# A planned kernel on one core: new planner constants, start times and nudges, with the same instructions

## The chip, the core and the metric

The kernel runs on one core of a Trainium2 chip. The metric is the device time of one execution in microseconds (us), as a median over runs. The engines are TensorE (PE, with its weight loads PEld), VectorE (DVE), ScalarE (ACT), GpSimd (POOL) and SyncE (SP, which here only issues DMAs; POOL issues some too).

## What is computed

A linear-attention block gated by a mixer MLP, for 2048 tokens of width 512, in float32:

```python
x = A_x
xn = _layernorm(x)
s = _A_ref(xn, wqkv, wo)                    # 32 heads of 16, linear attention
g = _silu(_B_ref(xn, w1, w2, w3, w4))       # token shifts and an MLP of 1376
return x + s * g
```

```python
# _A_ref: phi(t) = where(t > 0, t + 1, exp(t)) + 1e-6
kv = einsum("bhsd,bhse->bhde", phi(k), v); z = sum over s of phi(k)
o = einsum(phi(q), kv) / (einsum(phi(q), z) + 1e-6);  return o @ wo
# _B_ref
h = _gelu(_layernorm(x) @ w1)
hs = concat of the four column quarters of h, shifted by +1, -1, +2, -2 tokens, @ w2
x1 = x + hs
return x1 + _gelu(_layernorm(x1) @ w3) @ w4
```

## The kernel before

**Arithmetic.** Each float32 operand is split into a high and a low part for the PE's fp32r format, and each product is three matmuls (hi x hi, lo x hi, hi x lo). Names such as u_0h and u_0l or w_0h and w_0l are such pairs: usually ACT rounds the high part and DVE subtracts to get the low part. Large products are made in seven partial products instead of eight (function `seven`, L890): the banks `pa`, `pb` and `pe` are written by groups of six matmuls (two chunks of three), ACT or DVE takes the sum out, and the next group accumulates further into the same bank. So TensorE cannot go on in a bank before the reader of the last group is done; it computes other groups meanwhile. Functions that use this form are the second mixer product (`mix2`), the up and down products of the MLP (`up_pair`, which reads weight forms that `load_form` fetches from DRAM) and the products of q with kv and wo (`attend_pair`).

**Stages of the span.** From 0 to 44 us: k and q projections of the first tokens, Gram products for the row statistics, and the layernorm's fold into the weights; from 44 us `mix1` (L927, bank `h`: normalized x times w1, which needs the scaled weights w_0h and so on), then alternately k/q work, `mix2`, and later, block by block (four blocks of 512 tokens), the MLP (up, then down into bank `a`) and the attention. `chain` (L1324) adds the residual to a block's MLP sum, `gate` (L1430) makes silu, multiplies by the attention (`th`), adds x and stores.

The end of the head has this path: means are transposed on PE and written to DRAM as one row (`mrow`), fetched back spread over all partitions (`um`, SP), subtracted from x transposed (`xt`, DVE), and sums over it make the correction that DVE adds to the w1 weights (`w_s`); ACT rounds that to w_0h, and the first `h` matmul can start. The term w1 arrives in `w1t` by a load from SP and three accumulating gathers from POOL into the same tile. `rs` is a row of reciprocal roots, made on POOL by a power (`power`, L608/L611); `kr` on ACT reads it.

**What sets the order.** Nothing is written out by hand. The program code adds operations to a `Plan` (L88) in program order, each with its engine, its busy time, its latency, and what it reads and writes; `deadlines` and `backward` (L269) give each a due time from the nominal sequence of matmuls, and `emit` (L275) puts them out: it keeps a clock per engine and, again and again, takes the operation that can start first; among those within .02 us (PE) or .08 us (others) the one due first. It follows the tile slots (98 pieces, 8 PSUM banks), the port that DVE and POOL share, the loaded ACT table and, with `landing` (L228), when a DMA will have landed. These numbers only set the order of instructions on each engine, and which buffer a tile gets; on the chip the engines run by semaphores. A table `SOONER` (L1696) moves the due times of single operations, by number, in quarters of a us.

Lines that the rows below name: all matmuls are issued from L148, ACT from L170, DVE's tensor-tensor operations from L192, its scalar ones from L197 and L202, SP's loads from L212, its stores from L216, its fetches from L220, and POOL's gathers (DMAs that add into their target) from L224. In the changed file these lines stand at the same numbers up to L224, and up to six lines lower behind.

The rules of `emit` that the change touches (`r` is the time at which a reader `o` of the operation `op` is ready; the last line is from `landing`):

```python
free = {e: 0.0 for e in avail}
...
if o.eng == e == "PE" and not flow:
    r = 0.0
elif o.eng == e:
    r = op.end
else:
    r = op.end + self.GAP
...
dma = max(dma, s + (.33 if soft else 0)) + op.mb * op.rate
```

Of the kernel before, what the change touches and what calls it, by code (L numbers as in the profile page):

```python
# [14 lines left out]
P = 128  # L15
# [66 lines left out]

class Op:
    __slots__ = ("eng", "busy", "lat", "emit", "pre", "post", "tiles", "opens", "two", "table", "patience", "soon", "loads",
                 "nom", "due", "ready", "at", "end", "mb", "order", "rate")


class Plan:  # L88
# [9 lines left out]
    def add(self, eng, busy, lat, reads, writes, emit, two=False, table=None, mb=0.0):  # L98
        op = Op()
        op.eng, op.busy, op.lat, op.emit, op.two, op.table, op.mb = eng, busy, lat, emit, two, table, mb  # L100
        op.pre, op.post, op.tiles, op.opens = {}, [], {}, False
        op.order = len(self.ops)
        op.patience, op.soon, op.rate = self.patience, False, 0.0
# [55 lines left out]
    def act(self, out, src, func, scale=1.0, bias=None, total=None):  # L159
        nc = self.nc  # L160
        psum = out.tile.psum or src.tile.psum
        lat = (.15 if psum else .195) + out.n / 1200
        lat += .092 * (isinstance(scale, View) + isinstance(bias, View)) + (.095 if total is not None else 0)
        table = {AF.Exp: 0, AF.Gelu_apprx_tanh: 1, AF.Silu: 2}.get(func)

        def emit():
            kw = {} if bias is None else {"bias": get(bias)}
            if total is not None:
                kw["accum_out"] = total.get()
            nc.scalar.activation(out.get(), src.get(), func, scale=get(scale), **kw)  # L170

        self.add("ACT", lat - .1, lat, [src, scale, bias], [out] + ([] if total is None else [total]), emit, table=table)
# [31 lines left out]

    def move(self, eng, out, src, kind, mb, reads, writes, emit):
        op = self.add(eng, .42 if eng == "SP" else .6, 0, reads, writes, emit, mb=mb)
        op.rate = self.RATE[kind]
        return op

    def load(self, out, src):  # L210
# [11 lines left out]
    def gather(self, out, src, share=1.0):  # L222
        return self.move("POOL", out, src, "gather", out.n * P * 4 / 1e6 * share, [src, out], [out],
                         lambda: self.nc.gpsimd.dma_start(out.get(), get(src), accum_op=ALU.add))  # L224

    RATE = {"load": 2.92, "fetch": 3.5, "row": 4.18, "turn": 5.7, "store": 2.44, "gather": 5.79}

    def landing(self, op, s, dma):  # L228

        soft = op.eng == "POOL"  # L230
        dma = max(dma, s + (.33 if soft else 0)) + op.mb * op.rate
        late = min(1.11, .68 * max(0.0, dma - s))
        return dma, max(dma + (1.36 if soft else 1.25) + late, s + (3.77 if soft else 1.97 if op.loads else 1.68))

    GAP = .06
    PATIENCE = 2.5
    COLD, COLD_TILL = 1.84, 5.8
    SAFE = 2.0
# [30 lines left out]
    def backward(self):  # L269
        for op in reversed(self.ops):  # L270
            if op.eng != "PE":
                for o in op.post:
                    op.due = min(op.due, o.due - self.GAP - (6.0 + op.mb * 4 if op.mb else op.lat))

    def emit(self, first, lead, reserve, window, ahead, table=()):  # L275
        self.deadlines(first)
# [7 lines left out]
                avail[op.eng].append(op)  # L284
        pe = [op for op in ops if op.eng == "PE"]
        head = 0
        free = {e: 0.0 for e in avail}
        slots = {tag: [(0.0, i) for i in range(n)] for tag, n in self.counts.items()}
        port, dma = 0.0, 0.8
        lock = [(-1.0, -1.0)] * 8  # L290
        under = [0.0] * 8, [0.0] * 8
        table = 0
# [3 lines left out]
        while left:  # L296
# [5 lines left out]
            for e, cands in avail.items():  # L302
                picks = []
                low = INF
                for op in cands:
                    s = max(free[e], op.ready)
                    if op.mb:
                        s = max(s, under[e == "POOL"][0] + self.GAP)
                    if op.two and s < port:
                        s = port  # L310
                    if e == "POOL" and not op.mb and not op.two:
                        s = next((b + .02 for a, b in lock if a <= s < b), s)
                    if op.table is not None and op.table != table:
                        s = max(s, free[e] + 1.28)
                    ok = True
                    fresh = [t for t in op.tiles if t.ap is None]
                    for t in fresh:
                        if t.tag not in slots:
                            continue
                        q = slots[t.tag]  # L320
# [4 lines left out]
                        s = max(s, q[need - 1][0] + self.GAP)  # L325
                        if e == "PE":
                            if op is not front and (len(q) < 2 or op.nom - front.nom > ahead):
                                ok = False
                                break
                        elif t.tag in lead:  # L330
                            n = lead[t.tag] * (1.5 if len(q) > reserve[t.tag] else 1)
                            if t.tag == "p":
                                n = min(n, SCARCE * (len(q) - need + 1))
                            s = max(s, op.due + slip - n - t.early)
                    if not ok:
                        continue
                    if e == "PE" and op.nom - front.nom > window:
                        continue
                    q = s
                    if op.table is not None and op.table != table and op.due + slip < s:  # L340
                        q = s - 1.28
                    picks.append((q, s, op))
                    low = min(low, q)
                if not picks:
# [7 lines left out]
            s, op = best  # L352
# [30 lines left out]
            for o in op.post:  # L383
                flow = o.pre[op]
                if o.eng == e == "PE" and not flow:
                    r = 0.0
                elif o.eng == e:
                    r = op.end
                else:
                    r = op.end + self.GAP  # L390
                if op.mb:
                    r = max(r, min(r + self.SAFE, o.due + slip - o.lat - self.SAFE))
                o.ready = max(o.ready, r)
# [8 lines left out]
def linear_attn_gated_by_mixer(  # L402
# [744 lines left out]
    def load_form(b, s, name):  # L1147
# [6 lines left out]
        else:  # L1154
# [1 line left out]
            o = d * TH  # L1156
            pl.fetch(in2(t.f32), w4d[s + r * NS].cut(
                [(o, o + TH), (o + 512, o + 512 + TH)], 512,
                lambda ap, o=o: ap.rearrange("p (k w) -> p k w", k=2)[:, :, o:o + TH]))
        G4[b, s, name] = t.cols(0, TH), t.cols(TH, 512)  # L1160

    def load_group(b, s):
# [161 lines left out]
    def chain(b, n):  # L1324
# [8 lines left out]
        for k in (("11",), ("12",), ("21", "22"))[n]:  # L1333
# [1 line left out]
            o = h * 1024 + d * TH  # L1335
            x1 = x1d[b].cut([(o, o + TH), (o + 512, o + 512 + TH)], 512, lambda ap, h=h, d=d: quarter_of(ap, h, d))
            pl.act(e[k], t.all, AF.Copy)
            pl.gather(in2(e[k]), x1)

    def quarter_of(ap, h, d):  # L1340
        return ap[2 * h * P:2 * (h + 1) * P, d * TH:(d + 1) * TH].rearrange("(j p) c -> p j c", p=P)
# [88 lines left out]
    def gate(b, h, d, a, o=0, w=512, xr=None, whole=False):  # L1430
# [8 lines left out]
        pl.tt(th, th, so, ALU.mult)  # L1439
        j0, j1 = o // TH, (o + w) // TH  # L1440
        if xr is None:
            pl.gather(in2(th), quarter(x, b, h, d, j0, j1))
# [170 lines left out]
    for b in range(NQ):  # L1613
# [80 lines left out]
                gate(b, 1, 0, r, j * TH, TH, xr=xr[1, 0], whole=j > 0)  # L1694

    SOONER = (  # L1696
# [4 lines left out]
    )  # L1701
    pl.emit(first=6.0, lead={"p": 14.0, "w": 14.0}, reserve={"p": 20, "w": 1}, window=12.0,
            ahead=6.0, table=SOONER)
# [37 lines left out]
```

## Time and profile before

| | us |
|---|---|
| median of 3 runs | 510.47 (510.02 to 511.31) |
| the profiled execution | 510.98 |
| its span, first to last instruction | 509.2 |
| granted TensorE clock | 1.000 |
| DMA moved | 115.67 MB, 227 GB/s on average |

The profiled execution is one execution with a recorder on; every row below is from it. Row forms: in the timeline, start, duration, engine, line, operation, result <- operands, shapes, how many; in square brackets the idle time of the engine just before and what released it. A matmul's duration is modelled, and successive ones overlap: what it costs is the distance to the next start, 0.232 us for 512 columns and 0.118 us for 256 at full rate. A DMA row of SP or POOL is the issue, not the transfer. The span is 1.8 us shorter than the execution's time; the rest is start and end outside of the records.

### The profile page before, as it was taken

How to read it: one execution, taken by the hardware profiler on the slowest of the kernel's cores; microseconds unless marked ns; L12 is line 12 of the kernel's file. 1: busy time of each engine (PE TensorE's matmuls, PEld its weight loads, DVE VectorE, ACT ScalarE, POOL GpSimd, SP SyncE). 2: the span in 40 equal slices, each digit the busy share in tenths (PEclk: the TensorE clock that was granted, in tenths of full speed). 3: DMA queues.
4: the chain of work that ended last, by engine and by line, in shares of the span. 5: the costliest groups of instructions: out<-in, count | busy, mean ns of one | idle time of the engine just before them, and what ended most of it. 6: DMA issues, size and time to landing. Idle time of an engine off the chain costs nothing.

```text
span 509.2 us, 9828 instructions
## 1 busy us (share of the span) xinstructions
PE 500.7 (98%) x3287; PEld 453.0 (89%) x3287; DVE 443.6 (87%) x945; ACT 374.3 (74%) x756; POOL 106.6 (21%) x157
## 2 busy tenths in 40 slices
PE   8998999999999999999999999999999999999996
PEld 6776877898888888889999999999999999999996
DVE  5989999999699985999999996977789869999564
ACT  5899688765797785867767688846597667987561
POOL 1276402363243122021000020300030300032100
PEclk9999999999999999999999999999999999999999
DMA  7989956369994799989875989989699897899905
GB/s 266 315 172 216 306 172 166 65 148 285 273 312 105 220 308 217 255 215 313 297 229 171 309 260 310 215 213 242 228 213 294 199 236 216 270 226 256 246 7 122
DMA packets 90895, 115.67 MB, mean 227 GB/s; under 512 B 8800, under 2 KB 50044, under 8 KB 90844
## 3 DMA queue, kind: packets, MB, share of 16 engines
q1 hardware_dynamic: 78668, 98.00, 60.9%
q0 software_dynamic: 12176, 17.04, 21.2%
q8 instruction: 26, 0.43, 0.3%
q14 instruction: 25, 0.20, 0.1%
HBM read 73.70 MB, written 32.91 MB: 209 GB/s over the span
## 4 chain that ended last, share of the span: by engine, by line
PE 93%; DMA 3%; ACT 2%; DVE 1%; SPq 0%; issue 0%; ACTq 0%
PE a L148 15%; PE pb L148 11%; PE h L148 9%; PE g L148 7%; PE pbk L148 7%; PE acc L148 6%; PE pe L148 6%; PE pbm L148 5%; PE pbs L148 5%; PE uc L148 3%; PE pek L148 3%; PE pa L148 3%; PE pem L148 2%; PE pes L148 2%; PE k L148 2%; PE pak L148 2%
## 5 line engine op out<-in xcount | busy, mean ns | idle before, releaser
L224 POOL DMA_DIRECT2D th<-in_x x14 | 15.5, 1468 | 173.6 <-DMA w4t<-w_0h 60.6
L170 ACT ACT_TABLE_LOAD x26 | 33.4, 1283 | 5.8 <-DMA w4t<-w_1l 2.3
L224 POOL DMA_DIRECT2D e<-x1d x12 | 14.4, 1302 | 56.8 <-ACT e L170 27.1
L224 POOL DMA_DIRECT2D o<-x x16 | 13.8, 860 | 50.6 <-DVE o L192 35.5
L224 POOL DMA_DIRECT2D zacc<-kr x16 | 14.3, 894 | 44.2 <-DVE kr L202 21.3
L170 ACT ACTIVATE gf<-gf 128x256 f32<-128x256 f32 (+1 forms) x48 | 22.0, 466 | 0.5
L611 POOL TENSOR_TENSOR rs<-w,nhalf 128x4 f32<-128x4 f32 (+2 forms) x10 | 11.5, 1149 | 29.3 <-DVE w L197 28.4
L202 DVE SCALAR_TENSOR_TENSOR kr<-kt,kr 128x512 f32<-128x512 f32 x16 | 10.9, 686 | 5.8 <-ACT kt L170 5.8
L170 ACT ACTIVATE ht<-ht 128x512 f32<-128x512 f32 x16 | 9.6, 624 | 6.9 <-DVE ht L192 6.8
L170 ACT ACTIVATE th<-e 128x512 f32<-128x512 f32 (+1 forms) x12 | 7.2, 612 | 8.7 <-DVE e L192 8.7
L192 DVE TENSOR_TENSOR e<-a,e 128x512 f32<-128x512 f32 (+1 forms) x12 | 7.6, 663 | 6.7 <-PE a L148 6.7
L605 DVE BATCH_NORM_STATS2 st<-o 128x6 f32<-128x512 f32 x16 | 10.8, 685 | 3.1 <-DMA o<-x 3.1
L170 ACT ACTIVATE x<-x,nm,rs 128x512 f32<-128x512 f32 x16 | 12.9, 807 | 0.0
L192 DVE TENSOR_TENSOR th<-th,so 128x512 f32<-128x512 f32 (+1 forms) x17 | 10.7, 652 | 2.5 <-ACT th L170 2.5
L170 ACT ACTIVATE y<-o,nm,rs 128x512 f32<-128x512 f32 x16 | 12.1, 809 | 0.7 <-DVE nm L202 0.7
L202 DVE SCALAR_TENSOR_TENSOR pq<-pq,qr 128x512 f32<-128x512 f32 x12 | 8.1, 686 | 4.4 <-ACT pq L170 4.4
L170 ACT ACTIVATE p<-pb 128x256 f32<-128x256 f32 x20 | 7.5, 375 | 5.9 <-PE pb L148 5.8
L192 DVE TENSOR_TENSOR ht<-h,abc 128x512 f32<-128x512 f32 x16 | 11.0, 686 | 0.4 <-PE h L148 0.3
L192 DVE TENSOR_TENSOR gf<-u,pe 128x256 f32<-128x256 f32 x20 | 8.2, 412 | 3.5 <-PE pe L148 3.4
L202 DVE SCALAR_TENSOR_TENSOR pq<-pq,rd 128x512 f32<-128x512 f32 x16 | 11.0, 690 | 0.2
L170 ACT ACTIVATE p<-pe 128x256 f32<-128x256 f32 x20 | 7.6, 380 | 4.9 <-PE pe L148 4.9
L192 DVE TENSOR_TENSOR gf<-pa,p 128x256 f32<-128x256 f32 x20 | 8.3, 415 | 3.3 <-PE pa L148 3.2
(1820 smaller groups left out, 2362.1 us busy)
## 6 DMA issues: line engine op xcount, KB each, us to landing
w_s<-in_w SPq DMA_DIRECT2D x34, 256.0 KB, 4.4
w_t<-w4t SPq DMA_DIRECT2D x26, 256.0 KB, 5.3
w_b<-w4d SPq DMA_DIRECT2D x24, 256.0 KB, 4.7
x<-in_x SPq DMA_DIRECT2D x16, 256.0 KB, 5.4
zacc<-kr POOLq DMA_DIRECT2D x16, 256.0 KB, 5.1
o<-x POOLq DMA_DIRECT2D x16, 256.0 KB, 4.5
x1d<-o SPq DMA_DIRECT2D x16, 256.0 KB, 3.6
xt<-in_xt SPq DMA_DIRECT2D x15, 256.0 KB, 5.2
```

Source lines behind the costliest of these rows:

```text
L148: lambda: nc.tensor.matmul(out.get(), lhs.get(), rhs.get(), start=start, stop=stop, skip_group_check=more))
L170: nc.scalar.activation(out.get(), src.get(), func, scale=get(scale), **kw)
L192: self.vec(eng, out, [a, b], lambda: self.e(eng).tensor_tensor(out.get(), a.get(), b.get(), op=op), True)
L202: lambda: self.nc.vector.scalar_tensor_tensor(out.get(), a.get(), get(s), b.get(), op0=op0, op1=op1),
L224: lambda: self.nc.gpsimd.dma_start(out.get(), get(src), accum_op=ALU.add))
L605: pl.add("DVE", .62, .69, [xv], [st], lambda: nc.vector.bn_stats(st.get(), xv.get()))
L611: lambda: g.tensor_tensor(out.get(), src.get(), nh.get(), op=ALU.pow))
```

## The change

Only the planner's numbers and rules are changed. It adds no arithmetic and takes none away, and the operations that the program code adds are the same.

```diff
-        lat = (.15 if psum else .195) + out.n / 1200
+        lat = (.165 if psum else .195) + out.n / 1200
...
-        op.rate = self.RATE[kind]
+        op.rate, op.tail = self.RATE[kind], self.TAIL.get(kind, 0.0)
...
-    RATE = {"load": 2.92, "fetch": 3.5, "row": 4.18, "turn": 5.7, "store": 2.44, "gather": 5.79}
+    RATE = {"load": 2.93, "fetch": 3.3, "half": 4.27, "row": 4.23, "turn": 5.4, "store": 2.45,
+            "gather": 5.73, "quarter": 6.42}
...
-        return dma, max(dma + (1.36 if soft else 1.25) + late, s + (3.77 if soft else 1.97 if op.loads else 1.68))
-
-    GAP = .06
+        return dma, max(dma + (1.36 if soft else 1.25) + late, s + (3.77 if soft else 1.97 if op.loads else 1.68)) + op.tail
+
+    GAP = {"PE": .16, "ACT": .035, "DVE": .035, "POOL": .15, "SP": .035}
+    BEGIN = {"PE": 1.0, "ACT": 2.0, "DVE": .8, "POOL": .8, "SP": .75}
+    DMA0 = 2.2
+    TABLE = 1.41
+    TAIL = {"row": .95}
...
-                    op.due = min(op.due, o.due - self.GAP - (6.0 + op.mb * 4 if op.mb else op.lat))
+                    op.due = min(op.due, o.due - self.GAP[o.eng] - (6.0 + op.mb * 4 if op.mb else op.lat))
...
-        free = {e: 0.0 for e in avail}
+        free = dict(self.BEGIN)
...
-        port, dma = 0.0, 0.8
+        port, dma = 0.0, self.DMA0
...
-                        s = max(s, free[e] + 1.28)
+                        s = max(s, free[e] + self.TABLE)
...
-                elif o.eng == e:
+                elif o.eng == e and not flow:
                     r = op.end
                 else:
-                    r = op.end + self.GAP
+                    r = op.end + self.GAP[o.eng]
...
-            pl.gather(in2(e[k]), x1)
+            pl.gather(in2(e[k]), x1, kind="quarter")
...
     SOONER = (
-        9, 64, 23, 58, 119, -8, 132, 2, 183, 4, 269, -8, 291, 8, 333, 72, 336, 16, 357, 2, 394, -4, 412, -32,
...
+        23, 4, 35, 8, 49, 4, 55, 2, 61, 4, 131, 3, 132, -6, 143, 2, 181, 8, 183, 4, 211, 2, 256, 64, 273, -4,
...
```

`GAP` is the lag that the planner puts between the end of an operation and the start of one that reads it. It was .06 us for all; now it goes by the reader's engine, .16 for TensorE and .035 for ACT, DVE and SP, and it also holds between an operation and its reader on the same engine. `load_form`'s fetches are of the new kind "half", the gathers of `chain` and `gate` of the new kind "quarter". `TAIL` makes the rows that are spread over the partitions land .95 us later in the plan. `BEGIN` starts the engines' clocks at times of their own. The `SOONER` table goes from 37 pairs to 57, 12 of which are as before.

Three places show what the new order moves. The first is the start of SP's queue, where weights (wk_s, first factor of k) and x transposed (xt) are loaded. Before:

```order
L212 DMA xt_0_99<-in_xt 128x256
L212 DMA wk_s_105<-in_wqkv 128x512
L212 DMA xt_0_99<-in_xt 128x256
L212 DMA wk_s_113<-in_wqkv 128x512
L212 DMA xt_1_117<-in_xt 128x512
L212 DMA wk_s_123<-in_wqkv 128x512
L212 DMA xt_2_127<-in_xt 128x512
L212 DMA wk_s_131<-in_wqkv 128x512
L212 DMA xt_3_134<-in_xt 128x512
```

And in the changed kernel:

```order
L212 DMA xt_0_98<-in_xt 128x256 x2
L212 DMA wk_s_107<-in_wqkv 128x512
L212 DMA wk_s_112<-in_wqkv 128x512
L212 DMA xt_1_116<-in_xt 128x512
L212 DMA wk_s_122<-in_wqkv 128x512
L212 DMA xt_2_126<-in_xt 128x512
L212 DMA w1t<-in_w 128x512
L212 DMA wk_s_134<-in_wqkv 128x512
L212 DMA xt_3_136<-in_xt 128x512
```

The load of w1t now stands ahead of the last wk_s and the last xt. On POOL, at the same time of the program, the first of the w1t gathers stood alone ahead of the powers that make rs; in the changed kernel two stand there:

```order
L224 DMA w1t<-in_w 128x512 x2
L616 TENSOR_TENSOR rs_92<-w_315,nhalf 128x1
L616 TENSOR_TENSOR rs_92<-w_361,nhalf 128x2
L224 DMA w1t<-in_w 128x512
L719 CAST u_0h<-hal 128x2
```

DVE begins with wk_0h and wk_0l instead of u_0h and u_0l, which now come fourth and eighth. On ACT, the operations sq (sums of squares of x rows) move ahead: two stand ahead of wneg and one more ahead of kr.

The second place is on TensorE in the MLP of the last block: bank pe_0 of the first pair, from its group with yt13 to the next with yb223. Before:

```order
L148 MATMUL pe_0_6281<-yt13h,w_0_s0l 128x256
L148 MATMUL pb_0_6255<-yt23h,w_0_s0h 128x256
L148 MATMUL pb_0_6255<-yt23l,w_0_s0h 128x256
L148 MATMUL pb_0_6255<-yt23h,w_0_s0l 128x256
L148 MATMUL pb_0_6255<-yt23h,w_0_s0h 128x256
L148 MATMUL pb_0_6255<-yt23l,w_0_s0h 128x256
L148 MATMUL pb_0_6255<-yt23h,w_0_s0l 128x256
L148 MATMUL pe_0_6281<-yb223h,w_0_s1h 128x256
```

And in the changed kernel, the last rows of the same piece:

```order
L148 MATMUL pb_0_6257<-yt23h,w_0_s0h 128x256
L148 MATMUL pb_0_6257<-yt23l,w_0_s0h 128x256
L148 MATMUL pb_0_6257<-yt23h,w_0_s0l 128x256
L148 MATMUL pb_1_6306<-yb113h,w_1_ah 128x256
L148 MATMUL pb_1_6306<-yb113l,w_1_ah 128x256
L148 MATMUL pe_0_6281<-yb223h,w_0_s1h 128x256
```

Between the two groups that use pe_0 stood six matmuls, and now eight: two of the next pair's first group are drawn ahead.

The third place is the end of SP's queue, with the stores of the last gates (th300 and th301, th310 and th311 are the two halves of two row groups; xr is a loaded part of x, which th311 gets by a gather instead). Before:

```order
L216 DMA out_0<-th300_0_7150 128x2x256
L216 DMA out_0<-th311_0_7213 128x2x256
L216 DMA out_0<-th301_0_7249 128x2x256
L216 DMA out_0<-th310_0_7268 128x256
L216 DMA out_0<-th310_256_7284 128x256
```

And in the changed kernel:

```order
L216 DMA out_0<-th300_0_7153 128x2x256
L216 DMA out_0<-th301_0_7248 128x2x256
L216 DMA out_0<-th311_0_7212 128x2x256
L216 DMA out_0<-th310_0_7268 128x256
L216 DMA out_0<-th310_256_7284 128x256
```

The store of th301 has moved ahead of that of th311.

More of the change, by code (lines that the diff above doesn't have):

```diff
@@ L84 @@
     __slots__ = ("eng", "busy", "lat", "emit", "pre", "post", "tiles", "opens", "two", "table", "patience", "soon", "loads",
-                 "nom", "due", "ready", "at", "end", "mb", "order", "rate")
+                 "nom", "due", "ready", "at", "end", "mb", "order", "rate", "tail")
 class Plan:
@@ L102, in add @@
         op.order = len(self.ops)
-        op.patience, op.soon, op.rate = self.patience, False, 0.0
+        op.patience, op.soon, op.rate, op.tail = self.patience, False, 0.0, 0.0
         op.loads = any(isinstance(v, View) and v.tile.tag != "dram" for v in writes)
@@ L220, in fetch, with gather @@
                          lambda: self.nc.sync.dma_start(out.get(), src.get()))
-    def gather(self, out, src, share=1.0):
-        return self.move("POOL", out, src, "gather", out.n * P * 4 / 1e6 * share, [src, out], [out],
+    def gather(self, out, src, share=1.0, kind="gather"):
+        return self.move("POOL", out, src, kind, out.n * P * 4 / 1e6 * share, [src, out], [out],
                          lambda: self.nc.gpsimd.dma_start(out.get(), get(src), accum_op=ALU.add))
-    RATE = {"load": 2.92, "fetch": 3.5, "row": 4.18, "turn": 5.7, "store": 2.44, "gather": 5.79}
+    RATE = {"load": 2.93, "fetch": 3.3, "half": 4.27, "row": 4.23, "turn": 5.4, "store": 2.45,
+            "gather": 5.73, "quarter": 6.42}
     def landing(self, op, s, dma):
@@ L307, in emit @@
                     if op.mb:
-                        s = max(s, under[e == "POOL"][0] + self.GAP)
+                        s = max(s, under[e == "POOL"][0] + self.GAP[e])
                     if op.two and s < port:
@@ L324, in emit @@
                             break
-                        s = max(s, q[need - 1][0] + self.GAP)
+                        s = max(s, q[need - 1][0] + self.GAP[e])
                         if e == "PE":
@@ L340, in emit @@
                     if op.table is not None and op.table != table and op.due + slip < s:
-                        q = s - 1.28
+                        q = s - self.TABLE
                     picks.append((q, s, op))
@@ L1158, in load_form @@
                 [(o, o + TH), (o + 512, o + 512 + TH)], 512,
-                lambda ap, o=o: ap.rearrange("p (k w) -> p k w", k=2)[:, :, o:o + TH]))
+                lambda ap, o=o: ap.rearrange("p (k w) -> p k w", k=2)[:, :, o:o + TH]), "half")
         G4[b, s, name] = t.cols(0, TH), t.cols(TH, 512)
@@ L1441, in gate @@
         if xr is None:
-            pl.gather(in2(th), quarter(x, b, h, d, j0, j1))
+            pl.gather(in2(th), quarter(x, b, h, d, j0, j1), kind="quarter")
         else:
```

7 rows, old and new, of the table SOONER are left out of this document.

## The prediction

> **What bounds the kernel now.** I began with the head of the page and its chain of waits, to learn which engine a reordering has to serve.
>
> ```profile
> span 509.2 us, 9828 instructions
> PE 500.7 (98%) x3287; PEld 453.0 (89%) x3287; DVE 443.6 (87%) x945; ACT 374.3 (74%) x756; POOL 106.6 (21%) x157
> PE 93%; DMA 3%; ACT 2%; DVE 1%; SPq 0%; issue 0%; ACTq 0%
> ```
>
> TensorE is busy 500.7 of 509.2 us and makes 93% of the chain that ended last. The change adds and drops no arithmetic, so whatever it gains or loses lies in the other 8.5 us, or in steps of TensorE that a late neighbour has stretched (a stretched step still counts as busy). The windows show where the 8.5 us are; the columns are the stretch, its length, the busy time of PE, PEld, DVE, ACT and POOL with instructions, then the granted clock, the DMA share and GB/s.
>
> ```profile
> 1.00:8.90 7.90, 6.84 (x27) 5.28 (x27) 3.48 (x8) 3.70 (x8) 1.83 (x9) 1.00 0.78 235
> 8.90:41.40 32.50, 32.50 (x138) 25.43 (x139) 30.31 (x74) 29.64 (x59) 15.25 (x25) 1.00 0.87 246
> 41.40:44.30 2.90, 1.21 (x6) 0.34 (x4) 2.90 (x7) 2.27 (x5) 2.82 (x6) 1.00 0.94 178
> 225.00:504.30 279.30, 279.19 (x2172) 269.31 (x2170) 239.63 (x506) 200.09 (x428) 32.99 (x29) 1.00 0.84 233
> 504.30:509.20 4.90, 0.25 (x3) 0.04 (x1) 1.14 (x3) 0.38 (x1) 0.00 (x0) 1.00 0.49 162
> ```
>
> The holes are at the ends: 1.0 us before the first matmul, 1.06 us (7.90 less 6.84) before 8.90, 1.69 us (2.90 less 1.21) around 42 us and 4.65 us (4.90 less 0.25) behind the last matmul. In the 279 us of the fourth row TensorE is idle for 0.11 us. The granted clock is 1.00 throughout. The waits of TensorE name who ends the first holes (what waits, for whom, us in total, times, longest):
>
> ```profile
> PE h L148 <- ACT w_0h L170: 1.2, 1, 1.2
> PE warm L148 <- POOL ones L518: 1.0, 1, 1.0
> PE k L148 <- ACT u_1h L170: 1.0, 1, 1.0
> PE w1m L148 <- DVE w1ml L192: 0.5, 1, 0.5
> ```
>
> The wait of `warm` stays, since `ones` is the first real operation of POOL in both orders, and so does that of `k`: the load behind u_1h is the fifth on SP in both. Open to the change are the 0.5 + 1.2 = 1.7 us at 42 to 44 us, the tail, and stretched steps in between.
>
> **The head, 0 to 44.3 us.** Traced back from the wait of 1.21 us, the rows are:
>
> ```profile
> 33.03 4.88 DMA um<-mrow
> 37.93 0.69 DVE L192 TENSOR_TENSOR xt<-xt,um 128x512 f32<-128x512 f32 x1 [1.17 <-DMA um<-mrow]
> 42.88 1.89 DVE L202 SCALAR_TENSOR_TENSOR w_s<-w1m,w_s 128x512 f32<-128x512 f32 x3
> 43.60 0.63 ACT L170 ACTIVATE w_0h<-w_s 128x512 fp32r<-128x512 f32 x1 [0.62 <-DVE w_s L202]
> 44.29 0.49 PE L148 MATMUL h<-u_0h,w_0h 128*128 128x512 f32 x1 [1.21 <-ACT w_0h L170]
> ```
>
> DVE waits 1.17 us for the row of means (um), then works without a hole from 37.93 to 42.88, 4.95 us, until w_s can start; ACT follows, then TensorE. The same DVE operations stand between um and that w_s in the new order, so the head moves only as um lands earlier or later. Between 9 and 41 us ACT (29.64 of 32.50 us) and DVE (30.31) are nearly full, and they bring um about. Four edits touch this.
>
> First, SP puts a w1t load in seventh place, ahead of wk_s3 and xt_3. What one more load in that row costs I take from the distance of two that follow each other:
>
> ```profile
> 10.19 0.63 ACT L170 ACTIVATE wk_3h<-wk_s 128x512 fp32r<-128x512 f32 x1
> 10.87 0.64 ACT L170 ACTIVATE u_3h<-xt 128x512 fp32r<-128x512 f32 x1
> ```
>
> They start 0.68 us apart: the loads behind it, and ACT with them, come 0.68 us later. Second, DVE starts with wk_0h; u_0h and u_0l, which stood first, come fourth and eighth:
>
> ```profile
> 3.04 0.29 DVE L197 TENSOR_SCALAR u_0h<-xt 128x256 fp32r<-128x256 f32 x1 [3.04 <-DMA xt<-in_xt]
> 3.37 0.42 DVE L192 TENSOR_TENSOR u_0l<-xt,u_0h 128x256 fp32r<-128x256 f32 x1
> 8.88 0.69 DVE L192 TENSOR_TENSOR u_1l<-xt,u_1h 128x512 fp32r<-128x512 f32 x1
> ```
>
> Done at 3 us they fill time in which DVE has nothing else; later they take 0.29 + 0.42 = 0.71 us of its full stretch. The 1.17 us before um cover that; without the cover it would cost the 0.71. Third, TensorE computes the first k group whole, so it wants u_1l as its third matmul instead of its fifth: u_1l ends at 9.57, two full-width steps of 0.23 behind 8.90 reach 9.36, so about 0.2 us of new wait. It hides in the later 1.7 us, as any delay of TensorE before 42 us does.
>
> Fourth, and for the change, ACT's order. Three waits of it are in the rows:
>
> ```profile
> 14.26 0.60 ACT L170 ACTIVATE wneg<-ksum 128x512 f32<-128x512 f32 x1 [0.74 <-PE ksum L148]
> 19.30 0.60 ACT L170 ACTIVATE qneg<-qsum 128x512 f32<-128x512 f32 x1 [0.59 <-PE qsum L148]
> 20.81 0.73 ACT L170 ACTIVATE kr<-kt,rs 128x512 f32<-128x512 f32 x1 [0.91 <-POOL rs L611]
> ```
>
> The new order puts two operations ahead of wneg and one ahead of kr, so 0.74 + 0.59 = 1.33 us of the idle time can be filled. Less the 0.68 of the load this leaves 0.65 us by which the chain to um is earlier. DVE makes w1ml ahead of three of the xt, which takes the 0.5 us wait, but TensorE only arrives earlier at the next one, so nothing is counted for it. Where a price isn't shown (when w1t lands, whether the sq find their rows), the bounds are: all of the 0.68 and 0.71 arrives and the POOL wait of 0.91 grows by as much again, +2.3; both waits of 0.5 and 1.2 gone, −1.7, cut to −1.4 by the matmul that stands last before `h` in any order. **Term: −0.7, bounds −1.4 and +2.3**, nearer the lower end because the ACT rows are waits of the very operations that move.
>
> **Banks that TensorE comes back to, 60 to 500 us.** In the up, attend and mix2 stages a bank is written by six matmuls, read out by ACT or DVE, and accumulated into again. One such return, ACT between:
>
> ```profile
> 438.36 0.37 ACT L170 ACTIVATE p<-pe 128x256 f32<-128x256 f32 x1
> 438.45 0.28 PE L148 MATMUL pb<-yt23h,w_s0l 128*128 128x256 f32 x1
> 438.78 0.39 PE L148 MATMUL pe<-yb223h,w_s1h 128*128 128x256 f32 x1
> 439.00 0.28 PE L148 MATMUL pe<-yb223l,w_s1h 128*128 128x256 f32 x1
> ```
>
> Six other matmuls stand between; ACT starts 0.09 us before the last of them and ends at 438.73, TensorE goes on 0.05 later, and its steps are 0.33 and 0.22 instead of the 0.118 of an undisturbed one: 0.32 us lost, in steps that count as busy. This is a bad one; the groups show the mean (us in all, mean ns of one; an undisturbed one is the 0.28 us at 438.45):
>
> ```profile
> L148 PE MATMUL pbs<-m_t4h,q 128*128 128x256 f32 x32 | 7.5, 297 | 0.0
> L148 PE MATMUL pe<-yb223h,w_s1h 128*128 128x256 f32 x10 | 3.1, 312 | 0.1
> ```
>
> The first matmul of a return is 312 ns against 280, 0.032 us; half of the m_t4h are returns behind DVE, 17 ns over all and so 0.034 for each of these. Counted out of the two orders, 44 returns have six matmuls between in the old order and 7 in the new; 19 and 41 have seven, one step of 0.118 more cover. So 37 returns at 0.032 us are relieved: −1.2 if seven are enough; I take **−1.0**, as some of the seven-matmul returns will still be late. Bounds: if each relieved return saves as much in the next step as in its own, −2.4; if ACT and DVE come later by the same step, so that nothing is relieved and the 22 new returns of seven cost 0.02 each, +0.5.
>
> **Long waits where ACT stands in other work.** The 0.32 above is one of five of 0.16 to 0.32 us in the trace, behind 512-wide operations of ACT. The new order draws these anew: 0, and ±1.5 (about five of the size shown) for the range.
>
> **Table loads.** The planner now allows 1.41 us for one instead of 1.28.
>
> ```profile
> L170 ACT ACT_TABLE_LOAD x26 | 33.4, 1283 | 5.8 <-DMA w4t<-w_1l 2.3
> 439.54 1.28 ACT L170 ACT_TABLE_LOAD   x1
> 440.83 0.42 ACT L170 ACTIVATE f_0a<-gf 128x256 fp32r<-128x256 f32 x1
> ```
>
> The load ends at 440.82 and the next operation starts at 440.83. There are 26 in both orders; a plan that is 0.13 us pessimistic costs nothing by itself, since the engines run by semaphores and not by planned times. By the Trainium skill (ScalarE: Activation LUTs, What ACT_TABLE_LOAD costs) each switch of set pays some 1380 ns of drain besides the 1283 ns load; that would make even 1.41 far too short and every operation planned behind a load late. The trace agrees on the 1283 and shows 0.01 us in place of a drain, so the sum is left as it is.
>
> **The tail.** The last stores of the old order stand th300, th311, th301 on SP.
>
> ```profile
> SPq L216 <- DMA th<-in_x: 33.2, 7, 16.7
> 503.11 0.68 DVE L192 TENSOR_TENSOR th<-th,xr 128x512 f32<-128x512 f32 x1
> 504.32 2.25 SPq L216 DMA_DIRECT2D out<-th  x4
> 505.46 0.42 DVE L192 TENSOR_TENSOR th<-th,xr 128x256 f32<-128x256 f32 x1
> ```
>
> th301 is ready at 503.11 + 0.68 = 503.79, but the store of th311 ahead of it on the queue waits until 504.32 for its gather. Now th301 goes first, 0.53 us earlier, and what flows last is 256 KB shorter. If the end is set by the flow of these stores, all 0.53 comes back; if by the last piece, ready at 505.88 in both, nothing. The end is 509.20, 3.32 us behind that piece, and the queue took the stores until 506.57 (504.32 + 2.25): the flow counts. **Term −0.5, bounds −0.9 and 0.**
>
> **Sum.** −0.7 − 1.0 + 0 − 0.5 = −2.2 us. The profiled execution took 510.98 us (span 509.2 and 1.8 around it), 0.51 above the median of 510.47, so 508.8 against its own time and 508.3 against the median. The bounds are not all reached at once; the likeliest case's own range is 506.0 to 510.0.
>
> **Rivals.**
>
> *A: nothing that can be told apart.* The returns are relieved, and ACT's other work slides under them: the new busy-ACT waits take the +1.5 above, and −2.2 + 1.5 = −0.7 gives 509.8; with the tail at 0 as well, 510.3. For it speaks that the five long waits had other causes than the number of matmuls between; against it that they are few beside the 37. I name 510.3.
>
> *B: slower, through POOL's queue.* The new order issues two w1t gathers back to back ahead of the powers that give rs; both add into the same tile, so the second cannot go before the first has landed.
>
> ```profile
> 16.56 1.03 POOL L224 DMA_DIRECT2D w1t<-in_w  x1 [13.51 <-DMA w1t<-in_w]
> 24.57 0.91 POOL L224 DMA_DIRECT2D w1t<-in_w  x1
> ```
>
> If the w1t load lands at about 10.2 us (seventh in the row where the eighth feeds ACT at 10.19) and a gather takes until T, the second is issued at 10.2 + T and holds POOL for its 1.0 us, and the power takes about another. ACT's kr has its rs by 20.81 (above), so this decides from T = 8.6 us. In the old order the second gather is issued at 24.57, 8.0 us behind the first: T is under that there, with less of SP's traffic beside it. At T = 11, rs, kr (which already waits 0.91 us for it) and all behind come 2.4 us late; with DVE's 0.7 that is +3.1, and with the bank and tail terms −1.5 it is +1.6: 512.1 against the median. The Trainium skill (DMA: Bandwidth & Descriptors, Queues, rings and completion order) has each DMA engine alternate between the queues it has work for, packet by packet; by that a gather under SP's run of loads gets a share and T stretches, and SP's loads stretch with it. The windows above show a DMA share of 0.87 there and cannot show who yielded.
>
> *C: the order moves and TensorE doesn't.* The stretched steps are set by the engines' own lags and not by the distance; then only head and tail count, 510.47 − 1.2 = 509.3. It lies with A in what a measurement can tell.
>
> **How the numbers follow.** This kernel's measurement tells about 0.3% from no change, 1.5 us: faster is below 508.9, slower above 512.0. The forecast 508.3 gets 0.54, A and C 0.25, B 0.21. Part of the forecast's range lies above 508.9, and part of A's below; they are taken to cancel. The range of 506.0 to 512.4 holds the forecast's, A's, and B's central price.
>
> **What would show it.** Right: `h` starts before 43.8 us with DVE's wait for um below 0.8; the group pe<-yb223h,w_s1h comes under 295 ns; TensorE's span from `h` to its last matmul, 460.26 us here (504.30 + 0.25 − 44.29), falls by about 1; the end comes 4.1 us or less behind the last matmul (4.65 here). Wrong: a wait of ACT for POOL rs above 2 us near 20 us (B); new waits of TensorE above 0.3 us between 60 and 500 us, or the returns as long as before (A, C).

## The result

The changed kernel takes 508.20 us (median of 9 runs, 507.67 to 509.72) against 510.76 for the one before (9 runs, 509.52 to 513.21): the ratio is 0.9948, with a 95% interval of 0.9930 to 0.9967. It is faster by 0.5%, 2.6 us, which is more than the 0.3% that a measurement tells from no change. Forecast were 508.3 and 2.2 us.

The profiled execution of the changed kernel took 507.67 us. The head of its page and its chain:

```profile
span 505.9 us, 9830 instructions
PE 496.0 (98%) x3287; PEld 450.9 (89%) x3287; DVE 439.6 (87%) x945; ACT 375.4 (74%) x756; POOL 110.0 (22%) x157
PE 89%; ACT 6%; DMA 3%; DVE 1%; issue 1%; SPq 1%; ACTq 0%
```

TensorE is busy 4.7 us less with the same matmuls, so it was stretched steps that went, and the span is 3.3 us shorter. The two groups of bank returns that the prediction used (mean ns of one at the bar):

```profile
L148 PE MATMUL pbs<-m_t4h,q 128*128 128x256 f32 x32 | 7.0, 282 | 0.0
L148 PE MATMUL pe<-yb223h,w_s1h 128*128 128x256 f32 x10 | 2.8, 284 | 0.0
```

297 and 312 ns became 282 and 284, the length of a matmul that waits for nothing. TensorE's waits, though, have two new rows behind the head (the third and the sixth):

```profile
PE h L148 <- ACT w_0h L170: 1.3, 1, 1.3
PE warm L148 <- POOL ones L523: 1.0, 1, 1.0
PE pb L148 <- ACT p L170: 1.0, 1, 1.0
PE k L148 <- DMA wk_s<-in_wqkv: 0.9, 1, 0.9
PE qsum L148 <- DVE kt L202: 0.8, 1, 0.8
PE a L148 <- ACT gf L170: 0.6, 1, 0.6
```

By region, worked out from the start of `h` and the start and end of the last matmul (before: 44.29, 504.27, 504.55; after: 44.55, 501.37, 501.65):

| | before | after | change | forecast |
|---|---|---|---|---|
| head, to the first `h` | 44.29 | 44.55 | +0.26 | −0.7 |
| `h` to the last matmul's start | 459.98 | 456.82 | −3.16 | −1.0 |
| last matmul's end to the end of the span | 4.65 | 4.25 | −0.40 | −0.5 |

So the head missed its gain, the stretch behind it gained three times what was forecast, and the two errors oppose each other in the sum. The experiments ask where each row comes from.

### Where the head went

These rows of the changed kernel answer to the chain from um to `h`, to the moved operations of ACT (sq) and to POOL's queue:

```profile
14.17 0.63 ACT L170 ACTIVATE sq<-x 128x512 f32<-128x512 f32 x1 [0.67 <-DMA x<-in_x]
16.66 0.69 DVE L192 TENSOR_TENSOR wqt<-wqt,wq_s 128x512 f32<-128x512 f32 x1 [0.94 <-DMA wq_s<-in_wqkv]
17.44 0.64 ACT L170 ACTIVATE sq<-x 128x512 f32<-128x512 f32 x1 [0.93 <-DMA x<-in_x]
22.05 0.71 ACT L170 ACTIVATE kr<-kt,rs 128x512 f32<-128x512 f32 x1
31.58 0.33 SPq L220 DMA_DIRECT2D um<-mrow  x1
38.09 0.68 DVE L192 TENSOR_TENSOR xt<-xt,um 128x512 f32<-128x512 f32 x1
43.03 1.88 DVE L202 SCALAR_TENSOR_TENSOR w_s<-w1m,w_s 128x512 f32<-128x512 f32 x3
43.37 0.61 ACT L170 ACTIVATE kq_0h<-kq 128x512 fp32r<-128x512 f32 x1
43.89 0.61 ACT L170 ACTIVATE w_0h<-w_s 128x512 fp32r<-128x512 f32 x1
44.55 0.49 PE L148 MATMUL h<-u_0h,w_0h 128*128 128x512 f32 x1 [1.26 <-ACT w_0h L170]
9.97 1.03 POOL L224 DMA_DIRECT2D w1t<-in_w  x1 [6.95 <-DMA w1t<-in_w]
17.39 0.87 POOL L224 DMA_DIRECT2D w1t<-in_w  x1 [6.39 <-DMA w1t<-in_w]
```

um is asked for 1.45 us earlier than before (31.58 against 33.03), and DVE no longer waits for it. But DVE arrives at the first xt at 38.09, later than the 37.93 of before, because it is full ahead of it. From xt to w_s it takes 4.94 us (4.95 before).

DVE is not the last to come, though. Before, ACT stood idle for 0.62 us until w_s was there, and started w_0h 0.72 us behind the start of w_s (42.88 and 43.60). At that distance it could now have started at 43.75. It started at 43.89, without a wait, right behind kq_0h: ACT had other work until then. In the 21.2 us from 22.70 on it has no hole at all; before the change (first row) it had 0.97 us of holes (columns as in the prediction's windows):

```profile
22.70:43.90 21.20, 19.90 (x87) 15.17 (x85) 19.56 (x49) 20.23 (x39) 15.69 (x28) 1.00 0.77 168
22.70:43.90 21.20, 20.59 (x91) 16.11 (x89) 19.96 (x49) 21.20 (x42) 15.11 (x24) 1.00 0.59 161
```

The profile's own chain to `h` agrees. Before, it runs over mrow, um and DVE; in the changed kernel it runs along ACT from 21.3 us on, and ahead of that over DVE to a row of x that landed at 17.4. A second execution of the changed kernel, below, has the same chain. So ACT sets the head now, with DVE 0.14 us ahead of it.

Why ACT is no earlier stands in the same rows. The sq were to fill its waits for ksum and qsum, 0.74 and 0.59 us. Those shrank to nothing and 0.28. But the rows of x for the sq that moved ahead had not landed, and ACT waited 0.67 and 0.93 us for them; kr starts at 22.05, 1.24 us later than before. The second execution shows 0.68 and 0.92. This is read from rows; no experiment here moves the sq back.

### Where the two new waits come from

ACT and DVE around the two places, in order of time:

```profile
378.94 1.28 ACT L170 ACT_TABLE_LOAD   x1 [1.33 <-DVE sf_1a L192]
380.23 1.34 ACT L170 ACTIVATE pq<-qv,rs 128x512 f32<-128x512 f32 x2
382.52 0.36 ACT L170 ACTIVATE p<-pb 128x256 f32<-128x256 f32 x1
382.93 0.38 PE L148 MATMUL pb<-yt22h,w_s0h 128*128 128x256 f32 x1 [1.02 <-ACT p L170]
385.81 0.41 DVE L192 TENSOR_TENSOR gf<-pb,p 128x256 f32<-128x256 f32 x1
386.30 1.28 ACT L170 ACT_TABLE_LOAD   x1 [1.83 <-issue]
387.59 0.42 ACT L170 ACTIVATE f_2a<-gf 128x256 fp32r<-128x256 f32 x1
389.06 0.36 PE L148 MATMUL a<-yb112h,w_lh 128*96 128x256 f32 x1 [0.61 <-ACT gf L170]
```

ACT stands idle for 1.83 us and then loads its table only after DVE has made gf (385.81 + 0.41 = 386.22). The load reads nothing of gf, and elsewhere it runs ahead: the one for ht near 192 us ends 5.69 us before its activation starts. The compiled instructions show the difference (semaphores waited for in brackets; those of the load are a wait right ahead of it):

```
ACT_TABLE_LOAD [waits DMAHW5_49,DVE_49]
ACTIVATE f_2a_5505<-gf_7_5496 128x256 [waits PE_49]
```

An activation with one semaphore keeps it; of several, all but one stand in a wait ahead of the table load, which then holds ACT for 1.28 us in series with what was waited for. The planner counts the load as running meanwhile, before and after the change.

### The profile page after: what moved, and what is told of

Same layout as the page of the kernel before. It is cut to its first block, busy times and chain, and to the rows that moved or that the text cites. A ratio compares the mean times of both kernels' runs of the same rounds, so it can differ in the third digit from the quotient of the medians.

```text
span 505.9 us, 9830 instructions
## 1 busy us (share of the span) xinstructions
PE 496.0 (98%) x3287; PEld 450.9 (89%) x3287; DVE 439.6 (87%) x945; ACT 375.4 (74%) x756; POOL 110.0 (22%) x157
## 4 chain that ended last, share of the span: by engine, by line
PE 89%; ACT 6%; DMA 3%; DVE 1%; issue 1%; SPq 1%; ACTq 0%
PE a L148 15%; PE pb L148 11%; PE h L148 9%; PE g L148 7%; PE pbk L148 7%; PE acc L148 6%; PE pe L148 6%; PE pbs L148 4%; PE pbm L148 4%; PE pek L148 3%; PE uc L148 3%; PE pa L148 3%; PE pes L148 2%; PE pem L148 2%; PE pak L148 2%; DMA x<-in_x 1%
## 5 line engine op out<-in xcount | busy, mean ns | idle before, releaser
L616 POOL TENSOR_TENSOR rs<-w,nhalf 128x4 f32<-128x4 f32 (+2 forms) x10 | 10.1, 1006 | 34.4 <-DVE w L197 24.4
```

The costliest lines, as they stand in the source:

```text
L616: lambda: g.tensor_tensor(out.get(), src.get(), nh.get(), op=ALU.pow))
```

## The experiments

### Bank returns: the lag of TensorE alone, both ways

In the kernel before, one constant, with nudges fitted anew (`SOONER`, by the planner's clock):

```diff
-    GAP = .06
+    GAP = {"PE": .16, "ACT": .06, "DVE": .06, "POOL": .06, "SP": .06}
```

> The kernel before with one constant of the change alone: the lag of TensorE behind what it reads, .16 us instead of .06; the nudges are fitted anew by the planner's own clock until it shows 0.7 us of waits for TensorE. Between the two halves of a bank, six matmuls stand 3 times instead of 44. Theory (this lag relieves the returns): the groups pbs<-m_t4h and pe<-yb223h come to 286 ns or less (297 and 312 before, 282 and 284 in the changed kernel), and the time to 507 to 508.7. Rival (the other constants or the changed nudges do it): the groups stay above 295, the time at 510 to 511.

Measured: 510.96 us, ratio 0.9987 (0.9969 to 1.0005). The groups, and the longest wait of TensorE:

```profile
L148 PE MATMUL pbs<-m_t4h,q 128*128 128x256 f32 x32 | 7.0, 282 | 0.0
L148 PE MATMUL pe<-yb223h,w_s1h 128*128 128x256 f32 x10 | 2.9, 290 | 0.0
PE pe L148 <- ACT p L170: 1.1, 1, 1.1
```

The constant, with its fit, takes 297 to 282 ns and 312 to 290. The second is above the 286 expected, but far from 295. The time did not follow: this fit has the wait of 1.1 us and three of 0.2 to 0.3 behind the head, `h` to the last matmul is 459.5 us, and the tail is 5.7 us. Relief of the returns is worth its time only in an order without new long waits.

The other way, in the changed kernel, again with nudges fitted anew:

```diff
-    GAP = {"PE": .16, "ACT": .035, "DVE": .035, "POOL": .15, "SP": .035}
+    GAP = {"PE": .06, "ACT": .035, "DVE": .035, "POOL": .15, "SP": .035}
```

> The changed kernel with the lag of TensorE back at .06 us and everything else of the change kept; the nudges behind the head are fitted anew by the planner's own clock until it shows 0.3 us of waits. Six matmuls stand between the halves of a bank 53 times. Theory: the groups pbs<-m_t4h and pe<-yb223h are back at 295 ns or more, and the time at 510 to 512. Rival (the other constants do it): groups at 286 or less and 508.2 within 0.5.

Measured: 519.53 us, ratio 1.016 (1.0131 to 1.0188), with:

```profile
L148 PE MATMUL pbs<-m_t4h,q 128*128 128x256 f32 x32 | 7.4, 292 | 0.0
L148 PE MATMUL pe<-yb223h,w_s1h 128*128 128x256 f32 x10 | 3.0, 299 | 0.0
```

The losses are back in most part (292 is below the 295 expected). The time itself answers another question: in this fit one of the last gates is computed late, and 10.1 us pass after the last matmul instead of 4.25. From `h` to the last matmul it is 461.8 us, 5.0 more than in the changed kernel. So the lag is what relieves the returns, as both fits say, each with nudges of its own; no total of these two fits measures its worth.

### Table loads: an activation that lets the load go ahead

At two places, then at all 25 later loads (without the condition on `op.order`), the emission puts a one-element activation of the coming function ahead; it writes a small buffer of its own, and nothing else moves:

```diff
-            op.emit()
+            self.preload(op, table); op.emit()
...
+    def preload(self, op, table):
+        if op.table is not None and op.table != table and op.order in (4065, 4095):
+            fn = (AF.Exp, AF.Gelu_apprx_tanh, AF.Silu)[op.table]
+            self.nc.scalar.activation(self.spare.all.get(), self.seed[:, :1].get(), fn)
...
```

> The changed kernel, in the same order on every engine, with two activations added on ACT: one element wide, of the function that comes next, reading a constant, directly ahead of pq of the ninth q quarter and of f_2a22, so that the table load in front of them has no semaphore to wait for. Theory (the load waits for all but one of its activation's semaphores and then holds ACT for 1.28 us in series; this makes the two new long waits of TensorE near 382 and 388): the wait of 1.18 us falls to 0.4 to 0.7 and that of 0.77 to 0.1 or less, the time by 1.0 to 1.5 to about 507. Rival (what ACT waits for is late by itself): both waits stay within 0.2 and the time at 508.2.

Measured: 506.26 us, ratio 0.9895 (0.9870 to 0.9921). ACT at the two places, and TensorE between 378 and 390 us in the changed kernel and in this one (columns as in the prediction's windows):

```profile
378.32 1.28 ACT L249 ACT_TABLE_LOAD   x1
379.62 0.20 ACT L249 ACTIVATE spare<-ones 128x1 f32<-128x1 f32 x1
382.00 0.36 ACT L170 ACTIVATE p<-pb 128x256 f32<-128x256 f32 x1
383.96 1.28 ACT L249 ACT_TABLE_LOAD   x1
385.25 0.20 ACT L249 ACTIVATE spare<-ones 128x1 f32<-128x1 f32 x1
385.79 0.42 ACT L170 ACTIVATE f_2a<-gf 128x256 fp32r<-128x256 f32 x1 [0.33 <-PE a L148]
```

```profile
378.00:390.00 12.00, 10.37 (x86) 9.96 (x85) 9.18 (x20) 9.14 (x18) 0.00 (x0) 1.00 0.95 294
```

```profile
378.00:390.00 12.00, 12.00 (x102) 12.00 (x102) 10.80 (x26) 10.88 (x24) 0.00 (x0) 1.00 1.00 319
```

The loads now start 0.01 and 0.02 us behind ACT's previous operation, at 378.32 and 383.96. Both waits of TensorE are gone, the first altogether where 0.4 to 0.7 were expected to stay, and the time fell by 1.9 us, more than the 1.0 to 1.5 expected. The interval lies below that of the changed kernel: this version beats both. After `h` TensorE no longer has a wait in its table; from `h` to the last matmul it is 454.74 us, 5.2 less than before the change.

> The same activation ahead of all 25 later table loads; ten of them had a semaphore to wait for. Theory: no more than a few tenths of a us beyond the two, since the others hold up nothing that TensorE reads soon: 506.5 to 507.2. Rival (the added activations, some 0.2 us each on ACT, delay evictions): slower than with two alone, 507.5 or more.

Measured: 507.24 us, ratio 0.9916 (0.9885 to 0.9947). That lies between theory and rival. The interval overlaps that of two places alone and that of the changed kernel, so all 25 are told apart from neither; nothing is seen to be gained by the others.

### The end: the order of two stores, both ways

In `emit`, the store of th311 (operation 5450) is held back until that of th301 (5485) is out, in the kernel before; and the reverse in the changed one. No other row of any engine moves.

```diff
-                for op in cands:
+                for op in (c for c in cands if c.order not in HOLD or ops[HOLD[c.order]] in done):
```

> The kernel before with one row moved: the store of th301 ahead of that of th311; all other rows of every engine stand as before. Theory (the flow of the last stores sets the end): last matmul to the end of the span falls from 4.65 us to 4.1 to 4.3, as in the changed kernel (4.25), and nothing else moves. Rival (the last piece, ready in both at the same time, sets the end): 4.65 stays and the changed kernel's 0.4 us comes from somewhere else.

> The changed kernel with the old order of the last stores (th311 ahead of th301), all else the same. Theory (the order of the stores is worth 0.3 to 0.5 us at the end): last matmul to the end of the span 4.5 to 4.7 us, against 4.2 to 4.5 in the five runs with the new order. Rival (as the run with the swap in the kernel before suggests, 4.56 against 4.65): the order is worth 0.1, and 4.2 to 4.5 stays.

The span and the last matmul, in the first (the new order in the kernel before), then in the second (the old order in the changed kernel):

```profile
span 510.1 us, 9828 instructions
505.26 0.28 PE L148 MATMUL a4x<-w_9h,f_9l 128*128 128x256 f32 x1
```

```profile
span 507.8 us, 9830 instructions
502.92 0.28 PE L148 MATMUL a4x<-w_9h,f_9l 128*128 128x256 f32 x1
```

That is 4.56 us in the first (510.1 − 505.54), where 4.1 to 4.3 were expected, and 4.60 in the second, as expected. The spans are rounded to 0.1, so each value is good to 0.05. The old order shows 4.65, 4.71 and 4.60 in three executions; the new one, in seven executions of the changed kernel and of variants that keep its end, 4.25, 4.25, 4.29, 4.24, 4.19, 4.22 and once 4.51, and 4.56 in the kernel before. So in the changed kernel one execution with the old order speaks for some 0.3 us, while in the kernel before one execution gives the rival's answer, 0.1. Whether the order of these two stores makes the 0.4 us of the changed kernel stays open.

### The head: loads, start times, and the same kernels again

> The changed kernel with the w1t load on SP moved back by two places, behind wk_s3 and xt_3; TensorE, ACT and DVE have the same order as in the changed kernel. Theory (DVE sets the head now, and its wait of 0.94 us for a wq_s load is the load in front of it): that wait shrinks by up to 0.68 and h starts at 43.9 to 44.3 instead of 44.55. Rival 1 (ACT's own chain sets it): ACT's loads come earlier too, but h stays within 0.1 of 44.55. Rival 2 (the w1t gathers set it): they start later and h is later than 44.55.

> The changed kernel with the planner's start times and the first DMA time as in the kernel before (0 and 0.8 us); DVE then starts with u_0h and u_0l again, and the rest is planned anew from there. Theory (DVE sets the head, and 0.71 us of u_0h and u_0l in its full stretch are what it lost): h starts at 43.8 to 44.1. Rival (ACT or um sets it): 44.4 to 44.6.

> Both edits of the head together: the w1t load two places later, and the old start times. Theory: the two gains add, h starts at 43.2 to 43.7, 0.9 to 1.3 us earlier than in the changed kernel, and the time falls from 508.2 to about 507.2 if the rest stays. Rival (whatever starts earlier waits for the next thing in the head): 44.2 to 44.6 and 508.2 within its interval.

The first holds operation 419 (the w1t load) until 32 (xt_3) is out, with the line shown above; the second is

```diff
-    BEGIN = {"PE": 1.0, "ACT": 2.0, "DVE": .8, "POOL": .8, "SP": .75}
-    DMA0 = 2.2
+    BEGIN = {"PE": 0.0, "ACT": 0.0, "DVE": 0.0, "POOL": 0.0, "SP": 0.0}
+    DMA0 = 0.8
```

and the third has both. `h` started at 45.90, 46.18 and 44.61; the times were 511.65, 510.81 (one run each) and 509.25 (ratio 0.9965, 0.9945 to 0.9984). None of the starts that the theories expected came, and none of the three is faster than the changed kernel. Their common theory, that DVE sets the head, does not hold in the rows either: in all three w_0h starts without a wait, behind other work of ACT, and w_s had been done 0.17 to 0.25 us earlier. To know what such starts are worth, both kernels were profiled once more as they are.

> The changed kernel once more, to see what its rows do from one execution to the next. If the head is set by when the first loads land, h starts anywhere from 44.3 to 46.2 here; the two long waits near 382 and 388 come again within 0.2 us (1.18 and 0.77), since they are in the order, and the groups pbs<-m_t4h and pe<-yb223h at 281 to 286 ns. If instead the head was made later by the change, h starts at 44.4 to 44.7 again.

> The kernel before once more. h starts anywhere from 44.0 to 45.7 if the first loads set it, and at 44.2 to 44.4 if not; from h to the last matmul 459.5 to 460.2 (459.98 and 459.64 in two runs of this order); last matmul to the end 4.6 to 4.7; groups 295 to 298 and 310 to 314 ns.

The starts of `h`: the changed kernel again, the kernel before again, and the kernel before with the swapped stores, whose head is the same:

```profile
44.44 0.49 PE L148 MATMUL h<-u_0h,w_0h 128*128 128x512 f32 x1 [1.26 <-ACT w_0h L170]
```

```profile
43.38 0.49 PE L148 MATMUL h<-u_0h,w_0h 128*128 128x512 f32 x1 [1.21 <-ACT w_0h L170]
```

```profile
45.62 0.50 PE L148 MATMUL h<-u_0h,w_0h 128*128 128x512 f32 x1 [1.21 <-ACT w_0h L170]
```

One and the same head gives 43.38, 44.29 and 45.62 before the change (mean 44.43), and after it 44.55, 44.44 and, in the runs that leave the head alone (old order of stores, added activations), 45.77, 45.19 and 45.14 (mean 45.02). The spread is 2.2 us, so a difference of 0.6 between the means is nothing that can be told, and neither can the three experiments on the head. In these five of the new order, w_0h always starts without a wait behind other work of ACT, and in the three of the old one it always waits for w_s. What did come again: the two new waits (1.0 and 0.6 in the changed kernel's second profile), the groups (282 and 285 against 297 and 310), and `h` to the last matmul (457.2 and 457.2 against 459.6 and 460.8). The last value is above what was expected, 459.5 to 460.2: this execution has a wait of 0.5 us at 404 us that the other two of the order lack.

The w1t experiment showed one more thing. TensorE, ACT and DVE have the changed kernel's order there, yet `h` to the last matmul is 459.3 us: two more waits appear, of 0.9 and 0.7, the longer behind this row of ACT, where the changed kernel's second profile shows a wait of 0.34:

```profile
419.92 0.63 ACT L170 ACTIVATE q10h<-q10t 128x512 fp32r<-128x512 f32 x1 [1.52 <-DMA q10t<-q10d]
```

Ahead of the other, ACT waited 0.86 us for y_0t, for which it doesn't wait in the changed kernel. One execution can lose 2 us to two late transfers, so no single profile measures such a change.

## Why the prediction came out right, point by point

**The bound.** Right: TensorE bounds the kernel, and the gain lies in its stretched steps.

**The head, −0.7.** Wrong in its mechanism. The step that failed is the fourth edit, by which 1.33 us of ACT's idle time can be filled and the chain comes earlier: those waits nearly went, but the moved sq waited 0.67 and 0.93 us for their rows of x, which the prediction had named but left without a price. With it failed "the head moves only as um lands earlier or later": um was issued 1.45 us earlier, and neither DVE nor ACT, which were full, could use it; ACT now sets the head, by 0.14 us over DVE. Of the two prices set against the gain, the 0.71 for DVE can't be found: u_0h and u_0l stand ahead of a wait of 0.94 us (at 16.66), so DVE had the time. The 0.68 for the load is not told apart by the experiments. The mean of `h` is 0.6 us later, with a spread of 2.2 within one order: no gain, and a loss that can't be told from none.

**The returns, −1.0.** Right mechanism, size too small by a factor of three to five, and past its own bound of −2.4. Worked out from the starts of the 256-column matmuls (each step less its 0.118 us, summed over the step into a return and the one behind it), returns with six between lost about 2.2 us before, and those with seven to nine another 1.9; after, about 0.3 each. That is 3.5 us; the 5.1 below also hold what these returns don't account for. Two things were missed. The mean of 312 ns holds only a part of a return's loss: in the quoted case the step into it was longer by 0.21 and the step behind it by 0.10. And returns of seven to nine were taken as harmless, which they were not, in an order that placed the reader late. The new lag, .16, is about what the old rows show: 0.05 us from the end of ACT's p (438.73) to the start (438.78), and 0.10 in the step behind. With it the planner treats a late reader as a wait and finds another place for it.

**Long waits behind ACT, 0 ± 1.5.** The five went, and the changed order made two new ones, 1.18 and 0.77 us as steps, 1.95 in all and past the 1.5 of the range. This is rival A's mechanism, and it took back two fifths of the relief (5.1 = 3.16 + 1.95). Its cause was not the one that rival A named: ACT was not busy in other work but held by a table load in series with a semaphore.

**Table loads, no effect.** Right for the 1.41 as a number. Where the load stands against its activation's semaphores was not looked at, and that was worth 1.9 us. For the drain of some 1380 ns by the Trainium skill (ScalarE: Activation LUTs, What ACT_TABLE_LOAD costs) the changed kernel shows no room either: f_2a starts at 387.59 behind a load that ends at 387.58.

**The tail, −0.5.** Near in size: −0.40 between the two profiled executions. The mechanism, the flow of the last stores, is not shown: moving the two stores alone gave 0.3 us one way and 0.1 the other, in one execution each.

**Rivals C and B.** C is ruled out by the groups, which came down in every execution of the new order. B too: the second gather went 7.42 us behind the first (17.39 − 9.97), below the 8.6 from which it would decide, and kr at 22.05 waited for nothing. By the packet-wise sharing of the Trainium skill (DMA: Bandwidth & Descriptors, Queues, rings and completion order) the gather was to be stretched among SP's loads; here it took no longer than the 8.0 us of before.

**The sum.** −0.7 − 1.0 + 0 − 0.5 was forecast; the executions show about 0 to +0.6, −5.1, +1.95 and −0.4, which is −3.0 to −3.5, beside the 3.3 between the two profiled executions (510.98 and 507.67). The medians differ by 2.6: the profiled execution of the changed kernel is the fastest of its nine, 0.5 under its median, and that of before is 0.2 above its own. That 508.3 was met owes as much to luck as to the forecast: the new waits hid most of what the returns gave beyond it. The prediction's own signs are divided accordingly. Of the signs for it, DVE's wait for um went, the group came under 295 ns and the stretch from `h` shrank, but `h` did not start before 43.8 and the end did not come within 4.1 us; of the signs against it, the new waits above 0.3 us came.

## What to carry to other kernels

A stretched matmul costs more than its own length shows: count a bank return by the steps around it, and for every return, not only the shortest. When a wait on the path is taken away, ask for each engine on the chain whether it could go earlier, not only for the last one that waited, and whether the operations that are to fill a wait have their own data by then. Before a table load that must not wait, put a tiny activation without semaphores; and compare heads of one execution each only after the same kernel has shown what its head does from run to run.

## What the runs showed of the hardware

- A table load with semaphores ahead of it (its activation's, all but one) starts only when they are met: 1.83 us of idle ACT at 384.46 to 386.30, gone with an activation of 0.20 us ahead of it.
- The first `h` of one and the same order started between 43.38 and 45.62 us in three executions, without a change of the granted clock by more than 0.003.
